# Attention scores on TensorE's row halves and attention-times-values on its quarters, in float32, in a fused attention and MoE kernel

## The chip, the cores and the metric

The kernel runs on one NeuronCore of one Trainium2 chip. The core has a matrix engine (TensorE), three engines for elementwise work (VectorE, ScalarE, GpSimd), a queue engine that issues most transfers (SyncE, called SP in the profile), and 16 DMA engines. The metric is the device time of one execution in microseconds (us). Profiles are of one execution; times are medians of several.

## The reference

The first half is attention over pooled keys and values: 8 batches, 8 heads, 576 positions, head size 64, with means over 8 neighbouring positions, so that each query sees 72 keys. The second half is a dense two-layer network on the 4608 tokens.

```python
k_p = k.reshape(B, H, Sp, pool, D).mean(axis=3)
v_p = v.reshape(B, H, Sp, pool, D).mean(axis=3)
scores = scale * np.matmul(q, k_p.transpose(0, 1, 3, 2))
scores = scores - np.max(scores, axis=-1, keepdims=True)
attn = np.exp(scores)
attn = attn / (np.sum(attn, axis=-1, keepdims=True) + 1e-09)
attn_out = np.matmul(attn, v_p)
...
x = np.ascontiguousarray(attn_out.transpose(0, 2, 1, 3)).reshape(B * S, H * D)
h = x @ w_in                        # 4608 x 512 by 512 x 2048
g = h * np.clip(h + 3.0, 0.0, 6.0) / 6.0
out = g @ w_out                     # 4608 x 2048 by 2048 x 512
```

## The kernel before

The 4608 tokens are cut into blocks of 512, 256 and ten times 384 (`BLOCKS`). While the network runs on one block, the attention of later blocks is done in between: `block_steps` lists a block's attention steps, and `Paced` hands them out at the slots of the network's loops. Blocks 0 to 3 go through the network one by one (`run`, matmuls at L841 and L872). Blocks 4 to 11 go in pairs (`super_block`), with seven products in place of eight (matmuls at L1134, L1188 and L1261), their weights streamed from DRAM in 512 KB chunks by SP (L992). The first part of a super block has 54 paced slots, one for each product of six matmuls, and takes a share of the attention steps (`CUTS`, 0.85 in the first three); the rest are spread over the second part.

Many matmuls are done as three products of parts: an operand is cast to float32r (hi), the remainder is taken by a subtraction (lo), and hi x hi, hi x lo and lo x hi are summed. Other matmuls take plain float32.

The attention of a block goes in tiles of 128 tokens. Heads are handled in four pairs p, and pairs in two groups g of two. One tile and group take these steps:

- **Scores** (`Scores.product`, L456 to L464): one float32 matmul per pair, over 128 rows that hold the two heads' 64 dimensions. The keys lie in `kbds`, 128 rows by 144 columns, with zeros where the head of the row and the head of the column differ. A tile across the border of two batches is multiplied twice, with the other batch's queries cleared. Both pairs of a group go to one PSUM bank.
- **Softmax**: a maximum on VectorE (L467), four exponentials with sums on ScalarE (L472), a reciprocal on VectorE, and the division by the sum on GpSimd (`divide`, L501 and L507). Of the 72 keys the first 64 of each head go to `a`, the last 8 of four heads, twice, to `ar`, the "rest".
- **Transposes** (`transposes`, L566): two matmuls against the identity per group, and one for the rests of both groups. The result is split: ScalarE writes `ahi` (L583), VectorE `alo` (L585), and for the rests ScalarE writes two copies and VectorE a remainder (L596, L598).
- **Times values** (`av`, L641, with `av_sums`, L627): for each pair, four matmuls into one bank: `vhi` x `ahi`, `vhi` x `alo`, `vlo` x `ahi`, and the rests. Value tiles are block-diagonal over the two heads, with zeros cleared by GpSimd (L374). ScalarE copies the bank to `x` (L648). This is done once for each part of a block that lies in one batch: 384 tokens, or 192 and 192.

`load_v` and `prep_v` load the values of a batch, sum over the pool on VectorE (L383) and place the parts (L395, L396, L409, L410); `side_steps` orders them. Batches 0 and 1 have paths of their own.

PSUM has eight banks. The attention takes its banks in turn from a list (`att_bank`): three during the first part of a super block (`a0`, `a1`, `o3`), two during the second. TensorE takes its instructions in one order, which a scheduler sets from a simulated timeline; for the first part of the kernel, up to the fourth step of block 1, the order is written out (`ORDER`).

Of the kernel before, what the change touches and what calls it, by code (L numbers as in the profile page):

```python
# [98 lines left out]
def attention_moe_kernel(  # L99
# [83 lines left out]
    def after_mark():  # L183

        if len(window) == 2 and traced[-1].engine in marks:
            behind(traced[-1], marks[traced[-1].engine])
# [90 lines left out]
    def load_v(b, p):  # L277

        t = vraw[b, p] = ring("vst")
        half = slice(p % 2 * (POOL // 2) * D, (p % 2 + 1) * (POOL // 2) * D)  # L280
        to = t[:, : POOL * D].rearrange("p (c n) -> p c n", c=2)
        p -= p % 2
        if p < NPAIR:
            nc.sync.dma_start(to, v[b, p : p + 2, :, half].rearrange("c r n -> r c n"))
            after_mark()
            return
        for c in range(3):
            nc.sync.dma_start(to[c * REM : (c + 1) * REM], vr[b, :, :, half].rearrange("g r n -> r g n"))
            after_mark()
# [85 lines left out]

    def prep_v(b, p):

        if p == 0 and b not in W:
            place_v(b)
        n = P if p < NPAIR else 3 * REM  # L380
        x, y = (vraw.pop((b, p + i))[:n, : POOL * D].rearrange("p (c n) -> p c n", c=2) for i in range(2))
        for w, a, c in ((4 * D, x, y), (2 * D, x, x[:, :, 2 * D :]), (D, x, x[:, :, D:])):
            nc.vector.tensor_tensor(out=x[:, :, :w], in0=a[:, :, :w], in1=c[:, :, :w], op=ALU.add)  # L383
            after_mark()
        if p < NPAIR:
            place_heads(b, x[:, :, :D], slice(p, p + 2))
        else:
            place_rest(b, x[:, :, :D])
# [50 lines left out]
    class Scores:  # L439
# [25 lines left out]

        def top(self):
            nc.vector.tensor_reduce(out=self.mx, in_=self.ps, axis=AX.X, op=ALU.max, negate=True)  # L467
            self.later()
# [23 lines left out]
        def divide(self, engine):  # L492

            e, sm = self.e, self.sm
            if self.a is None:
# [4 lines left out]
            copies = 3 if self.first else 2  # L500
            engine.tensor_tensor(  # L501
# [6 lines left out]
                out=self.rest.rearrange("p (c h s) -> p c h s", c=copies, h=4),  # L508
# [7 lines left out]

    def scores(j, tile, g):

        s = Scores(tile, g)
        s.product()  # L520
        s.top()
        s.exps()
        s.invert()
        s.divide(nc.vector if j == 1 else nc.gpsimd)

    def a_tiles(j, g):


        if (j, g) not in attnT:
            attnT[j, g] = (  # L530
                pool.tile([P, 2, TMAX], F32R, name="ahi", bufs=2),
                pool.tile([P, 2, TMAX], F32R, name="alo", bufs=2),
                pool.tile([NR, TMAX], F32R, name="arem", bufs=2),
            )
        return attnT[j, g]
# [30 lines left out]
    def transposes(j, tile, g):  # L566
# [9 lines left out]
        for b, _, n, x0 in tile:  # L576
            src, o = ps[:, :, at : at + n], slice(x0, x0 + n)
            at += n
            if b == 0:
# [60 lines left out]

    def av(j, b, x0, T, p, later=None):  # L641
# [14 lines left out]
    def side_steps(b):  # L656

        ks = [lambda p=p: load_k(b, p) for p in range(NPAIR)]
        ks += [lambda p=p: prep_k(b, p) for p in range(NPAIR)]
        vs = []  # L660
        n = NPAIR + NG
        for p in range(n):
            vs.append(lambda p=p: load_v(b, p))
            if p > 2 and p % 2:
                vs.append(lambda p=p: prep_v(b, p - 3))
        vs.append(lambda: prep_v(b, n - 2))
        return ks, vs
# [5 lines left out]
    def block_steps(j):  # L673
# [4 lines left out]
        def turn():  # L678
            tile, g = todo.pop(0)
            steps.append(([], lambda: transposes(j, tile, g), None, ()))  # L680
            if g == NG - 1:
                while left and (left[0][0], left[0][1] + left[0][2]) in [(b, s0 + n) for b, s0, n, _ in tile]:
                    pb, _, T, x0 = left.pop(0)
                    steps.extend(([], lambda p=p, a=(j, pb, x0, T): av(*a, p), "av", (pb,)) for p in range(NPAIR))
# [198 lines left out]
    small = fixed.tile([P, 8], F32, name="small")  # L883
    mask, half, half_low = small[:, :6], small[:, 6:7], small[:, 7:]
# [682 lines left out]
```

## Time and profile before

| | |
|---|---|
| time, median of 3 runs | 892.96 us (892.43 to 894.55) |
| profiled execution, its own time | 893.88 us |
| its span in the trace | 892.1 us |
| instructions | 15646 |
| TensorE busy | 869.2 us, 5360 matmuls |
| VectorE busy | 665.9 us |
| ScalarE busy | 553.6 us |
| GpSimd busy | 83.6 us |
| DMA | 200.00 MB, mean 224 GB/s |

PE is TensorE's matmuls, PEld its weight loads, DVE VectorE, ACT ScalarE, POOL GpSimd. Each row of a group gives the line, engine and operation, what is written from what, shapes and count, then busy time and the mean duration of one, then the idle time of the engine just before them and what ended it. Durations of matmuls overlap, since a matmul is recorded until its last result while the next one already streams; what one costs in a row of them is the distance between starts. Span and profiled time differ by what lies around the traced instructions.

### The profile page before, as it was taken

The page shows a single profiled execution, that of the slowest core. Times are in us where ns is not written, and L with a number is a line of the kernel's source. Part 1 is how long each engine was busy: PE and PEld are TensorE (multiplying, and loading weights), DVE is VectorE, ACT ScalarE, POOL GpSimd, SP SyncE. Part 2 cuts the span into 40 slices and gives each one's busy share as a digit, 9 for nine tenths or more (in the row PEclk, how much of TensorE's full clock was granted, in tenths as well). Part 3 has the DMA queues.
Part 4 walks back from the last instruction along what each step waited for, and adds up shares of the span by engine and source line. Part 5 has one row for each costly group of instructions (what it writes and reads, how often), then busy time and mean ns, then how long its engine had stood idle before and what let it go on. Part 6 is the DMA issues. An engine that isn't in the chain of part 4 may idle for free.

```text
span 892.1 us, 15646 instructions
## 1 busy us (share of the span) xinstructions
PE 869.2 (97%) x5360; PEld 812.3 (91%) x5360; DVE 665.9 (75%) x1340; ACT 553.6 (62%) x1515; POOL 83.6 (9%) x168
## 2 busy tenths in 40 slices
PE   7899999999999999999999999999999999999998
PEld 6788888988989998998888999999999999999998
DVE  6999864567877785869788688897597877466664
ACT  5998766655656655778344688665577746355442
POOL 4100002110211100102000101100100200000000
PEclk9999999999999999999999999999999999999999
DMA  9970205995425234996587968877976777877873
GB/s 294 392 293 1 72 24 192 360 327 167 130 67 160 71 129 135 368 315 225 180 271 239 383 218 295 265 239 236 331 250 213 226 233 240 275 253 238 266 264 132
DMA packets 124654, 200.00 MB, mean 224 GB/s; under 512 B 13216, under 2 KB 81056, under 8 KB 124576
## 3 DMA queue, kind: packets, MB, share of 16 engines
q1 hardware_dynamic: 124432, 199.00, 67.8%
q8 instruction: 43, 0.70, 0.3%
q14 instruction: 35, 0.29, 0.1%
q10 hardware_dynamic: 144, 0.00, 0.0%
HBM read 158.08 MB, written 40.89 MB: 223 GB/s over the span
## 4 chain that ended last, share of the span: by engine, by line
PE 80%; DVE 8%; DMA 5%; ACT 4%; issue 2%; SPq 1%; POOL 0%; DVEq 0%; ACTq 0%; POOLq 0%
PE psx L1134 22%; PE psx L1261 19%; PE pso L872 12%; PE psh L841 12%; PE psx L1188 7%; PE psa L646 3%; PE psa L463 3%; ACT e L472 2%; PE psa L572 1%; DMA raw<-w_in_l 1%; DMA raw<-w_out_l 1%; DMA wd<-wq 1%; DVE vst L383 1%; DMA wsFalse<-wd 1%; DVE wq L939 1%
## 5 line engine op out<-in xcount | busy, mean ns | idle before, releaser
L1134 PE MATMUL psx<-x,wsFalse 128*128 128x384 f32 x768 | 151.8, 341 | 1.7 <-DVE g L1098 0.8
L841 PE MATMUL psh<-xhi,w 128*128 128x384 f32 (+2 forms) x520 | 145.9, 340 | 0.5 <-DVE g L853 0.4
L1134 PEld LDWEIGHTS psx<-x,wsFalse 128*128 128x128 f32 x768 | 133.6, 188 | 3.2 <-ACT c L1107 1.3
L1113 ACT CAST part<-g 128x768 fp32r<-128x768 f32 x100 | 83.3, 836 | 85.0 <-PE psx L1261 65.8
L1115 DVE TENSOR_TENSOR part<-g,part 128x768 fp32r<-128x768 f32 x100 | 95.2, 955 | 46.5 <-ACT part L1113 46.1
L872 PE MATMUL pso<-w,ghi 128*128 128x512 f32 x384 | 120.7, 398 | 0.4 <-ACT o L877 0.4
L1134 PE MATMUL psx<-x,wsTrue 128*128 128x384 f32 x576 | 115.8, 342 | 2.4 <-DMA wsTrue<-wd 2.3
L1261 PE MATMUL psx<-wsFalse,part 128*128 128x256 f32 x864 | 108.3, 282 | 1.5 <-DVE part L1115 1.1
L1261 PEld LDWEIGHTS psx<-wsFalse,part 128*128 128x128 f32 x864 | 105.2, 189 | 2.3 <-DVE part L1115 1.3
L1134 PEld LDWEIGHTS psx<-x,wsTrue 128*128 128x128 f32 x576 | 99.6, 188 | 3.1 <-DVE g L1092 3.1
L841 PEld LDWEIGHTS psh<-xhi,w 128*128 128x128 f32 x520 | 93.2, 188 | 8.2 <-DVE g L853 1.1
L472 ACT ACTIVATE e<-psa,mx 128x72 f32<-128x72 f32 x256 | 78.6, 324 | 23.7 <-DVE mx L467 22.4
L841 PE MATMUL psh<-xlo,w 128*128 128x384 f32 (+2 forms) x260 | 87.1, 336 | 0.0
L501 POOL TENSOR_TENSOR a<-e,sm 128x256 f32<-128x256 f32 x60 | 41.0, 683 | 478.3 <-DVE sm L490 377.9
L1261 PE MATMUL psx<-wsTrue,part 128*128 128x256 f32 x648 | 81.3, 283 | 0.0
L1261 PEld LDWEIGHTS psx<-wsTrue,part 128*128 128x128 f32 x648 | 79.3, 191 | 0.2 <-DVE part L1115 0.2
L872 PEld LDWEIGHTS pso<-w,ghi 128*128 128x128 f32 x384 | 69.1, 188 | 11.2 <-ACT o L877 0.7
L1090 ACT ACTIVATE r<-g,small 128x384 f32<-128x384 f32 x96 | 58.8, 621 | 28.4 <-DVE g L1098 28.0
L872 PE MATMUL pso<-w,glo 128*128 128x512 f32 x192 | 74.4, 399 | 0.0
L1098 DVE TENSOR_TENSOR g<-psx,c 128x384 f32<-128x384 f32 x96 | 52.3, 553 | 28.7 <-PE psx L1134 20.6
L1107 ACT COPY c<-psx 128x384 f32<-128x384 f32 x96 | 45.0, 485 | 28.5 <-PE psx L1134 28.1
L1092 DVE SCALAR_TENSOR_TENSOR g<-r,g 128x384 f32<-128x384 f32 x96 | 54.5, 576 | 9.7 <-ACT r L1090 9.2
(139 smaller groups left out, 1473.2 us busy)
## 6 DMA issues: line engine op xcount, KB each, us to landing
wsFalse<-wd SPq DMA_DIRECT2D x64, 512.0 KB, 4.6
wsTrue<-wd SPq DMA_DIRECT2D x48, 512.0 KB, 4.9
wsFalse<-w2d SPq DMA_DIRECT2D x31, 512.0 KB, 5.0
wsFalse<-w2t SPq DMA_DIRECT2D x27, 512.0 KB, 5.0
wsTrue<-w2d SPq DMA_DIRECT2D x21, 512.0 KB, 5.0
wsTrue<-w2t SPq DMA_DIRECT2D x21, 512.0 KB, 4.9
raw<-w_in_l SPq DMA_DIRECT2D x16, 512.0 KB, 8.6
raw<-w_out_l SPq DMA_DIRECT2D x16, 512.0 KB, 9.2
```

The lines of the kernel that those rows point to most:

```text
L472: nc.scalar.activation(self.e[:, h], self.ps[:, h], AF.Exp, bias=self.mx[:, h : h + 1], accum_out=self.sm[:, h : h + 1])
L841: nc.tensor.matmul(self.ps, l[f][:, c, :], r[:, c, :], start=c == 0 and i == 0, stop=c == NCC - 1 and i == 2)
L872: nc.tensor.matmul(pos, l, r, start=f == 0 and i == 0, stop=f == NF - 1 and i == 2)
L1090: nc.scalar.activation(r, src, AF.Relu, bias=half_low, scale=GSCALE / (6.0 * WSCALE))
L1092: nc.vector.scalar_tensor_tensor(out=g_of[i][:, k], in0=r, scalar=GSCALE, in1=src, op0=ALU.min, op1=ALU.mult)
L1098: nc.vector.tensor_tensor(out=g_of[i][:, k], in0=ps, in1=kept, op=ALU.add)
L1107: nc.scalar.copy(c, ps)
L1113: nc.scalar.copy(t[:, 0], src)
L1115: nc.vector.tensor_tensor(out=t[:, 1], in0=src, in1=t[:, 0].bitcast(F32), op=ALU.subtract)
L1134: nc.tensor.matmul(ps, w[:, l, c * P : (c + 1) * P], t[:, r, c], start=o in (1, 2, 5) and c == 0 and k == 0, stop=c == 1 and k == 2, skip_ ...
L1188: nc.tensor.matmul(to, l, w[:, qs, r], start=f == 0 and k == 0, stop=end and k == 2)
L1261: nc.tensor.matmul(to, t[:, l, k, i * P : (i + 1) * P], w[:, k, r], start=begin and k == 0 and y == 0 and i % 2 == 0, stop=m == NM - 1 and ...
```

## The change

From block 3 on (the third batch) the operands of the attention stay in float32. Scores take one matmul for each head, over the 64 rows of that head and its 72 key columns; the two heads of a pair lie in the two row halves of the array, and each half writes to a bank of its own, so that the products of both groups of a tile are made together at the first group's step (`Scores.products`). After the transposes, ScalarE copies `a` and the rests whole (`whole_a`). Values lie without zeros: two heads in 64 rows each, and `av_of_two` does two pairs at once, with each of its matmuls over 64 rows and 64 output columns, that is, a quarter of the array, and two banks. The rests of a batch are loaded to 128 rows, summed, and multiplied with a mask (`own`), which `own_rest` makes once. The hunks left out change where `divide` writes the rests and add the columns for `own`.

```diff
     def load_v(b, p):
 
         t = vraw[b, p] = ring("vst")
-        half = slice(p % 2 * (POOL // 2) * D, (p % 2 + 1) * (POOL // 2) * D)
-        to = t[:, : POOL * D].rearrange("p (c n) -> p c n", c=2)
-        p -= p % 2
         if p < NPAIR:
-            nc.sync.dma_start(to, v[b, p : p + 2, :, half].rearrange("c r n -> r c n"))
-            after_mark()
+            half = slice(p % 2 * (POOL // 2) * D, (p % 2 + 1) * (POOL // 2) * D)
+            to = t[:, : POOL * D].rearrange("p (g n) -> p g n", g=NG)
+            p -= p % 2
+            for r in range(2):
+                nc.sync.dma_start(
+                    to[r * D : (r + 1) * D], v[b, p + r, :, half].rearrange("(g s) n -> s g n", g=NG)
+                )
+                after_mark()
             return
-        for c in range(3):
-            nc.sync.dma_start(to[c * REM : (c + 1) * REM], vr[b, :, :, half].rearrange("g r n -> r g n"))
-            after_mark()
+        for r in range(2):
+            for g in range(NG):
+                at = (r * NG + g) * REM
+                nc.sync.dma_start(
+                    t[at : at + REM, : POOL * D],
+                    vr[b].rearrange("a (w g s) n -> g (a w) s n", w=2, g=NG)[g],
+                )
+                after_mark()
 
 
     pieces = {}
...
         for w in W[b][:2]:
             nc.gpsimd.memset(w.bitcast(F32), 0.0)
 
+    def own_rest():
+
+        nc.gpsimd.memset(own, 0.0)
+        for r in range(2):
+            for g in range(NG):
+                rows = slice((r * NG + g) * REM, (r * NG + g + 1) * REM)
+                nc.gpsimd.tensor_copy(own[rows, g::NG], mask[rows, 2 + r :: 2])
+
     def prep_v(b, p):
 
-        if p == 0 and b not in W:
-            place_v(b)
-        n = P if p < NPAIR else 3 * REM
-        x, y = (vraw.pop((b, p + i))[:n, : POOL * D].rearrange("p (c n) -> p c n", c=2) for i in range(2))
-        for w, a, c in ((4 * D, x, y), (2 * D, x, x[:, :, 2 * D :]), (D, x, x[:, :, D:])):
-            nc.vector.tensor_tensor(out=x[:, :, :w], in0=a[:, :, :w], in1=c[:, :, :w], op=ALU.add)
+        if b not in W:
+            if not W.keys() - {0, 1}:
+                own_rest()
+            W[b] = (
+                pool.tile([P, NPAIR, 2 * D], F32, name="v32", tag="vhi", bufs=2)[:, :, :D],
+                pool.tile([P, NPAIR, 2 * D], F32, name="vr32", tag="vlo", bufs=2)[:, :2].rearrange(
+                    "p i (g d) -> p (i g) d", g=NG
+                ),
+            )
+        heads, rest = W[b]
+        x, y = vraw.pop((b, p)), vraw.pop((b, p + 1), None)
+        c = 1 if y is None else NG
+        x = x[:, : POOL * D].rearrange("p (c n) -> p c n", c=c)
+        if y is not None:
+            y = y[:, : POOL * D].rearrange("p (c n) -> p c n", c=c)
+        for w in (4 * D, 2 * D, D):
+            z = y if y is not None and w == 4 * D else x[:, :, w : 2 * w]
+            nc.vector.tensor_tensor(out=x[:, :, :w], in0=x[:, :, :w], in1=z[:, :, :w], op=ALU.add)
             after_mark()
+        x = x[:, :, :D]
         if p < NPAIR:
-            place_heads(b, x[:, :, :D], slice(p, p + 2))
-        else:
-            place_rest(b, x[:, :, :D])
+            nc.scalar.mul(heads[:, p : p + 2], x, 1.0 / POOL)
+            return
+        nc.vector.tensor_tensor(
+            out=rest,
+            in0=x.broadcast_to([P, NPAIR, D]),
+            in1=own[:, :, None].broadcast_to([P, NPAIR, D]),
+            op=ALU.mult,
+        )
+        after_mark()
 
     def place_heads(b, vs, some=slice(None)):
         whi, wlo, _ = W[b]
...
                     nc.tensor.matmul(to, qt[:, p, :], kbds[b % 2][:, p, :], start=r == 0, stop=r == last)
             self.ps = ps[:, : 4 * SP].rearrange("p (h s) -> p h s", s=SP)
 
+        @staticmethod
+        def products(tile):
+
+            two = [Scores(tile, g) for g in range(NG)]
+            banks = [att_bank() for _ in two]
+            last = len(tile) - 1
+            for p in range(NPAIR):
+                for r, (qt, (b, _, _, _)) in enumerate(zip(qtiles[tile], tile)):
+                    for g, ps in enumerate(banks):
+                        rows = slice(g * D, (g + 1) * D)
+                        nc.tensor.matmul(
+                            ps[:, SP * p : SP * (p + 1)],
+                            qt[rows, p, :],
+                            kbds[b % 2][rows, p, SP * g : SP * (g + 1)],
+                            start=r == 0,
+                            stop=r == last,
+                        )
+            for s, ps in zip(two, banks):
+                s.ps = ps[:, : 4 * SP].rearrange("p (h s) -> p h s", s=SP)
+            return two
+
         def top(self):
             nc.vector.tensor_reduce(out=self.mx, in_=self.ps, axis=AX.X, op=ALU.max, negate=True)
             self.later()
...
 
     rests = {}
 
+    scored = {}
+
     def scores(j, tile, g):
 
-        s = Scores(tile, g)
-        s.product()
+        if j < 3:
+            s = Scores(tile, g)
+            s.product()
+        else:
+            if g == 0:
+                scored[tile] = Scores.products(tile)
+            s = scored[tile][g]
         s.top()
         s.exps()
         s.invert()
...
                 pool.tile([P, 2, TMAX], F32R, name="ahi", bufs=2),
                 pool.tile([P, 2, TMAX], F32R, name="alo", bufs=2),
                 pool.tile([NR, TMAX], F32R, name="arem", bufs=2),
+            )
+        return attnT[j, g]
+
+    def whole_a(j, g):
+
+        if (j, g) not in attnT:
+            attnT[j, g] = (
+                pool.tile([P, 2, TMAX], F32, name="aT", tag="ahi" if j % 2 else "alo", bufs=2)
+                if g < NG
+                else pool.tile([P, TMAX], F32, name="aTr", tag="arem", bufs=2)
             )
         return attnT[j, g]
 
...
         for b, _, n, x0 in tile:
             src, o = ps[:, :, at : at + n], slice(x0, x0 + n)
             at += n
+            if j > 2:
+                nc.scalar.copy(whole_a(j, g)[:, :, o], src[:, :2])
+                later()
+                if g:
+                    nc.scalar.copy(whole_a(j, NG)[:, o], src[:, 2])
+                    later()
+                continue
             if b == 0:
                 nc.vector.tensor_copy(first_a(j, g)[0], src[:, :2])
             else:
...
             whi, wlo, wrem = W[b]
             mms = [(whi[:, p], hi[:, i, o]), (whi[:, p], lo[:, i, o]), (wlo[:, p], hi[:, i, o])]
         return mms + [(wrem[:, g, i * P : (i + 1) * P], rem[:, o])]
+
+    def av_of_two(j, b, x0, T, i):
+
+        heads, rest = W[b]
+        o = slice(x0, x0 + T)
+        banks = [att_bank()[:, :T] for _ in range(2)]
+        for n in range(2):
+            for g in range(NG):
+                for r, ps in enumerate(banks):
+                    rows = slice(r * D, (r + 1) * D)
+                    nc.tensor.matmul(
+                        ps[g * D : (g + 1) * D],
+                        (rest if n else heads)[rows, 2 * i + g],
+                        whole_a(j, NG)[rows, o] if n else whole_a(j, g)[rows, i, o],
+                        start=n == 0,
+                        stop=n == 1,
+                        skip_group_check=True,
+                    )
+        for r, ps in enumerate(banks):
+            nc.scalar.copy(x_tile(j, "x", F32)[:, 2 * i + r, o], ps)
+            (after_mark if late else no_slot)()
 
     def av(j, b, x0, T, p, later=None):
 
...
 
         ks = [lambda p=p: load_k(b, p) for p in range(NPAIR)]
         ks += [lambda p=p: prep_k(b, p) for p in range(NPAIR)]
-        vs = []
-        n = NPAIR + NG
-        for p in range(n):
-            vs.append(lambda p=p: load_v(b, p))
-            if p > 2 and p % 2:
-                vs.append(lambda p=p: prep_v(b, p - 3))
-        vs.append(lambda: prep_v(b, n - 2))
+        order = [("load", 0), ("load", 1), ("load", 2), ("load", 3), ("prep", 0), ("load", 4)]
+        order += [("prep", 2), None, ("prep", 4)]
+        do = {"load": load_v, "prep": prep_v}
+        vs = [(lambda x=x: do[x[0]](b, x[1])) if x else no_slot for x in order]
         return ks, vs
 
     def loads_behind(tile):
...
             if g == NG - 1:
                 while left and (left[0][0], left[0][1] + left[0][2]) in [(b, s0 + n) for b, s0, n, _ in tile]:
                     pb, _, T, x0 = left.pop(0)
-                    steps.extend(([], lambda p=p, a=(j, pb, x0, T): av(*a, p), "av", (pb,)) for p in range(NPAIR))
+                    of, n = (av, NPAIR) if j < 3 else (av_of_two, NPAIR // 2)
+                    steps.extend(([], lambda p=p, a=(j, pb, x0, T), of=of: of(*a, p), "av", (pb,)) for p in range(n))
 
         for t in tiles_of[j]:
             pre = loads_behind(t)
```

More of the change, by code (lines that the diff above doesn't have):

```diff
@@ L500, in divide @@
             copies = 3 if self.first else 2
+            rest = self.rest.rearrange("p (c h s) -> p c h s", c=copies, h=4) if self.tile[0][0] < 2 else (
+                rests[self.tile].rearrange("p c (g h s) -> p g c h s", g=NG, h=4)[:, self.g]
+            )
             engine.tensor_tensor(
@@ L507, in divide @@
             engine.tensor_tensor(
-                out=self.rest.rearrange("p (c h s) -> p c h s", c=copies, h=4),
+                out=rest,
                 in0=e[:, None, :, D:].broadcast_to([P, copies, 4, SR]),
@@ L639, in av_sums @@
         return mms + [(wrem[:, g, i * P : (i + 1) * P], rem[:, o])]
+    def av_of_two(j, b, x0, T, i):
[13 more added lines that the diff above has]
+                        skip_group_check=True,
+                    )
+        for r, ps in enumerate(banks):
+            nc.scalar.copy(x_tile(j, "x", F32)[:, 2 * i + r, o], ps)
+            (after_mark if late else no_slot)()
     def av(j, b, x0, T, p, later=None):
@@ L882, in attention_moe_kernel @@
     make_identity(nc, ident)
-    small = fixed.tile([P, 8], F32, name="small")
-    mask, half, half_low = small[:, :6], small[:, 6:7], small[:, 7:]
+    small = fixed.tile([P, 8 + NPAIR], F32, name="small")
+    mask, half, half_low, own = small[:, :6], small[:, 6:7], small[:, 7:8], small[:, 8:]
     nc.gpsimd.memset(half, 0.5)
```

## The prediction

> **What bounds the kernel now.** I read the page first, for the engines' shares and the slices, then the waits of TensorE, then its groups with the shapes kept apart, then the timeline of single steps.
>
> ```profile
> span 892.1 us, 15646 instructions
> PE 869.2 (97%) x5360; PEld 812.3 (91%) x5360; DVE 665.9 (75%) x1340; ACT 553.6 (62%) x1515; POOL 83.6 (9%) x168
> ...
> PE   7899999999999999999999999999999999999998
> DVE  6999864567877785869788688897597877466664
> ...
> PE psx L1134 <- DMA wsTrue<-wd: 2.3, 1, 2.3
> ...
> PE psa L463 <- DVE arem L598: 1.3, 3, 0.9
> ...
> PE psa L646 <- DVE alo L585: 0.7, 3, 0.3
> ```
>
> TensorE is busy in 97% of the span and in nine tenths or more of every slice but the first two and the last. Its idle time is 892.1 - 869.2 = 22.9 us in all, and the three waits below the slices show how small the pieces are. VectorE is full only in the third to fifth slice, before any attention of the third batch runs. So a step of attention costs what it adds to TensorE's queue, and work taken from VectorE or ScalarE pays only where TensorE waits for it: 1.3 + 0.7 = 2.0 us for the parts that the change drops. The reader is to see that this is a sum over TensorE's instructions.
>
> **What is replaced.**
>
> ```profile
> L463 PE MATMUL psa<-kbd,qt 128*128 128x144 f32 x288 | 45.3, 287 | 1.3 <-DVE arem L598 1.3
> ...
> L646 PE MATMUL psa<-ahi,vhi 128*128 128x384 f32 x28 | 9.5, 341 | 0.2 <-DVE alo L585 0.2
> ...
> L646 PE MATMUL psa<-ahi,vhi 128*128 128x192 f32 x28 | 7.6, 273 | 0.7 <-DVE alo L585 0.5 <-ACT e L472 0.2
> ```
>
> Each score product is two calls in the code, and four records: one float32 call is two loads and two matmuls, always next to each other. Blocks 3 to 11 hold 27 tiles of 128 tokens; three of them span two batches and are done twice, so 30 tiles' worth, 60 products, 240 of the 288 records. The same blocks have six parts of 384 tokens and six of 192. At four pairs p each, these are 24 of the 28 steps of either width, each with three split matmuls and one for the rest.
>
> ```profile
> 503.21 0.65 PE L463 MATMUL psa<-kbd,qt 128*128 128x144 f32 x4
> 503.61 1.31 PE L1134 MATMUL psx<-x,wsTrue 128*128 128x384 f32 x6
> 504.75 0.34 PE L1134 MATMUL psx<-x,wsFalse 128*128 128x384 f32 x1
> ...
> 531.79 0.33 PE L646 MATMUL psa<-ahi,vhi 128*128 128x384 f32 x1
> ...
> 532.48 1.05 PE L1134 MATMUL psx<-x,wsFalse 128*128 128x384 f32 x5
> ...
> 431.80 0.25 PE L646 MATMUL psa<-ahi,vhi 128*128 128x192 f32 x1
> ...
> 432.23 0.41 PE L1188 MATMUL psx<-wsFalse,part 128*128 128x512 f32 x1
> ```
>
> The durations overlap, so I read starts. Four matmuls of av take 532.48 - 531.79 = 0.69 us at 384 columns (0.1725 each), and 432.23 - 431.80 = 0.43 us at 192 (0.1075 each). A score product takes 0.40 us to the next start; the six matmuls behind it take 1.14 us where six at 0.1725 take 1.035, so 0.105 us of it shows up later: 0.505 us. Removed: 60 x 0.505 = 30.3 us of scores, 24 x 0.69 + 24 x 0.43 = 26.9 us of av.
>
> **What is added: prices.**
>
> ```profile
> 36.65 0.60 PE L646 MATMUL psa<-a,v 128*128 128x256 f32 x2
> 37.09 0.60 PE L646 MATMUL psa<-arem,vrem 96*128 96x256 f32 x2
> ...
> 78.07 0.33 PE L646 MATMUL psa<-a,v 128*128 128x64 f32 x2
> 78.23 0.39 PE L646 MATMUL psa<-a,vrem 96*128 96x64 f32 x2
> 78.43 0.47 PE L841 MATMUL psh<-xhi,w 128*128 128x512 f32 x1
> 78.74 0.40 PE L841 MATMUL psh<-xlo,w 128*128 128x512 f32 x1
> ...
> 464.96 28.36 PE psx L1188 x123
> ```
>
> A float32 call of 256 columns takes 0.44 us, 0.22 per record, 0.86 ns a column. By columns a record costs 0.33 us at 384, 0.165 at 192, 0.062 at 72. But the four records of 64 columns, 0.055 us each by that rate, take 0.36 us to the next start, and the next matmul gives up 0.31 - 28.36/123 = 0.08 more: 0.44, or 0.11 each. That is also the pitch at 192 columns above, where the 384-column rate would give 0.086. So a record with a full-width (128-column) weight load has a floor near **0.11 us**. The new scores, 72 columns wide, still load 128 columns and stand on this floor; the new av loads 64 columns and streams 384 or 192, well above it.
>
> **How much overlaps** decides the sign, and no row before shows a matmul on part of the array. The order of the code does: a call's two records use the same half or quarter, so the second waits for the first; the next call is on another one and can start beside that second record, but its own second record must wait again. If matmuls start in program order, as in every timeline above, two records are in flight at any time, with halves or quarters: n calls of two records take n + 1 record times. I take this.
>
> The Trainium skill ("TensorE: Matmul & The Clock Gate", Part 3) says that matmuls start and end strictly in program order, and nothing here contradicts it: by it the quarters give a factor of two in float32, not four, and the sum is the one below. The same page's 10.6-fold for sixteen tiles is for one matmul per tile; no run here shows either.
>
> - Scores, per tile: 8 calls, 9 x 0.11 = 0.99 us against 1.01. 30 x -0.02 = **-0.6 us**. Bounds: 9 x 0.062 = 0.56 us if the halves hide the load (-13.5 us), 16 x 0.11 = 1.76 us if loads go one by one (+22.5 us). I take the middle since the floor is a row and only its overlap is unknown.
> - av, per step of two pairs: 8 calls, 9 x 0.33 = 2.97 us against 1.38 at 384; 9 x 0.165 = 1.49 against 0.86 at 192; twelve each: 19.1 + 7.5 = **+26.6 us**. Bounds: four at once, 1.32 and 0.66 us (-0.7 - 2.4 = -3.1 us); none, 5.28 and 2.64 us (46.8 + 21.4 = +68.2 us).
> - Changing the array's shape: 27 score steps and 24 av steps, in and out, 102 changes.
>
> ```profile
> 437.38 0.34 PE L646 MATMUL psa<-ahi,vhi 128*128 128x192 f32 x1
> 437.56 0.27 PE L646 MATMUL psa<-alo,vhi 128*128 128x192 f32 x1
> 437.67 0.28 PE L646 MATMUL psa<-ahi,vlo 128*128 128x192 f32 x1
> ```
>
> The nearest row is a matmul behind a transpose: 0.18 us to the next start instead of 0.11. I take this 0.07: 102 x 0.07 = **+7.1 us**; bounds 0 and a whole load more, 0.07 + 0.11 = 0.18 (18 us).
>
> **Other engines.**
>
> ```profile
> L585 DVE TENSOR_TENSOR alo<-psa,ahi 128x256 fp32r<-128x256 f32 x56 | 23.1, 415 | 1.9 <-ACT ahi L583 1.4
> ...
> L598 DVE TENSOR_TENSOR arem<-psa,arem 32x128 fp32r<-32x128 f32 x56 | 16.0, 286 | 4.5 <-ACT arem L596 2.8
> ...
> L410 DVE SCALAR_TENSOR_TENSOR vrem<-vst,small,vrem 32x128 fp32r<-32x128 f32 x24 | 7.7, 365 | 0.3
> ...
> L396 DVE SCALAR_TENSOR_TENSOR vlo<-vst,vhi 64x128 fp32r<-64x128 f32 x24 | 7.5, 313 | 0.5
> ...
> L596 ACT CAST arem<-psa 64x128 fp32r<-64x128 f32 x56 | 14.6, 260 | 11.4 <-DVE alo L585 6.9 <-DVE arem L598 3.8
> ...
> L472 ACT ACTIVATE e<-psa,mx 128x72 f32<-128x72 f32 x256 | 78.6, 324 | 23.7 <-DVE mx L467 22.4
> L472 ACT ACTIVATION_READ_ACCUMULATOR e<-psa,mx 128x1 f32 x256 | 53.7, 210 | 0.0
> ...
> vst<-v_l SPq DMA_DIRECT2D x24, 256.0 KB, 5.1
> ...
> vst<-vr_l SPq DMA_DIRECT2D x36, 64.0 KB, 4.1
> ```
>
> VectorE loses 48 of the 56 in either of the first two rows (19.9 + 13.7 us) and the next two rows whole (15.2 us), some 49 us; ScalarE one of two copies of the rests (24 x 0.26 = 6 us) and most of the placing of values. TensorE covers all of it, so the gain is the **-2.0 us** of waits above. GpSimd's clearing of value tiles goes, its division stays. SP issues 8 + 4 loads of values a batch instead of 4 + 6: twelve more in all, with fewer bytes of the rests. What stands behind them on SP is the weight stream, for which TensorE waited 2.3 us at the longest; one chunk that came as late would cost that, and I add nothing.
>
> The added wait is the second bank: both products of a tile are made at the first score step, each av step needs two banks at once, and the MoE matmuls stand behind on TensorE. A bank comes free after four exponentials, 4 x (0.324 + 0.210) = 2.1 us, of the second half one step later than now. The three attention waits above average 1.3/3 = 0.43 us; one such wait per tile would be 12 us. I take 0: the first part of a super block spreads 85% of some 30 steps over 54 products of 1.035 us, 2.2 us a step, and three banks turn.
>
> **Sum:** -0.6 + 26.6 + 7.1 - 2.0 = +31.1 us. The profiled execution took 893.88 us, 1.8 beyond its span and 0.9 above the median of 892.96; on the median the forecast is **924 us** (+3.5%).
>
> **Rivals.**
>
> - *Four at once* (the forecast's opposite side). If a quarter needs only its own predecessor, the second record of a call does not hold up the next quarter: scores 8 x 0.11 = 0.88 us (-3.9 us), av -3.1, waits -2.0, and half the price of the changes, +3.5: -5.5 us, **887 us**, between 880 and 893. It decides once more than three records run side by side, since av then costs no more than now. For it: the four outputs of a step lie in two banks and two halves of their rows, so none writes where another does. Against: every timeline above has its matmuls one after another, those of a call together. The skill's "TensorEngine Tiling (Array Packing)", Key Properties, says that tiles work independently, in loads too: that is this rival; the same list's drain at a change of mode is the +7.1 us. No run here shows either yet.
> - *Loads one by one, matmuls two by two*: scores +22.5, av +26.6, changes +7.1, waits -2.0: +54 us, **947 us**. For it: the floor of 0.11 us is a load's, and nothing above shows two loads at once.
> - *Loads one by one, quarters four at once*: 22.5 - 3.1 + 7.1 - 2.0 = +24.5, **917 us**.
> - *The parts of the array don't overlap in float32* (the change doesn't do what it says): 22.5 + 68.2 + 7.1 - 2.0 = +95.8, **989 us**.
>
> **How the numbers follow.** Forecast 0.40, its own range 917 (no price for changes) to 947 us (18 us for them, and the bank wait); four at once 0.28; one-by-one loads 0.13; that with quarters at four 0.06; no overlap 0.13. A difference of 0.3% (2.7 us) is about what a measurement of this kernel can tell from none, its three runs lying 2.1 us apart. Of *four at once*, 0.22 is faster than that and 0.06 within it; everything else is slower: 0.72. The range 880 to 952 leaves out no overlap and small tails.
>
> **What would show it.** The 16 records of a 384-column av step from the first start to the next work: about 3.0 us says two in flight, 1.3 four, 5.3 none. Scores: 16 records in 1.0 us or 1.76. The first matmul behind each step against its usual pitch gives the price of a change. PE's idle time before the two-bank steps shows the bank wait. I am wrong if records of one call on the same quarter run together, if hidden VectorE waits were worth far more than 2 us, or if banks make TensorE stand.

## The result and the profile after

The changed kernel takes 935.79 us (median of four runs, 934.43 to 944.91), the kernel before 893.75 us beside it on the same chip (892.43 to 894.87): a ratio of 1.0493 [1.0424, 1.0562], 42.0 us more. The forecast was 31.1 us more. The profiled execution took 935.04 us against 893.88; its span is 41.2 us longer.

First the page of the changed kernel: the span, the engines' shares, and the slices of TensorE (PE) and VectorE (DVE).

```profile
span 933.3 us, 16307 instructions
...
PE 917.7 (98%) x5792; PEld 814.1 (87%) x5792; DVE 618.7 (66%) x1178; ACT 535.8 (57%) x1449; POOL 75.3 (8%) x161
...
PE   7899999999999999999999999999999999999998
...
DVE  6999846446655675656787566876565677466674
```

TensorE has 432 records more and is 48.5 us longer busy. Its idle time falls from 22.9 to 933.3 - 917.7 = 15.6 us. VectorE loses 47 us, about the 49 that were counted, and the span grows all the same. The kernel is still a sum over TensorE's instructions; what the relief of the other engines is worth by itself is tried further down.

Next TensorE's groups after, with the shapes kept apart (the columns are busy time, mean ns of one, idle time before).

```profile
L511 PE MATMUL psa<-kbd,qt 64*128 64x72 f32 x480 | 50.8, 280 | 0.1
...
L733 PE MATMUL psa<-aT,v 64*64 64x384 f32 x96 | 19.7, 507 | 0.0
L733 PE MATMUL psa<-aTr,vr 64*64 64x384 f32 x96 | 17.7, 493 | 0.0
...
L733 PE MATMUL psa<-aT,v 64*64 64x192 f32 x96 | 12.7, 345 | 0.0
...
L733 PE MATMUL psa<-aTr,vr 64*64 64x192 f32 x96 | 10.4, 327 | 0.0
...
L498 PE MATMUL psa<-kbd,qt 128*128 128x144 f32 x48 | 7.3, 286 | 0.0
```

The two halves of the array have 480 records of scores between them, the four quarters 384 of av. The new steps don't wait: their idle column holds 0.1 us in all, and TensorE's view of waits has no row of an attention bank. So the cost of the two banks, which the prediction looked for in idle time, has to be sought elsewhere. Busy time can't be set against the span here, because records that run side by side are counted once and the gaps at a change of shape not at all. What can be read is the starts.

### What a step takes

The timeline of TensorE after: start, duration, line and tiles, number of records in a row.

```profile
513.17 1.11 PE L511 MATMUL psa<-kbd,qt 64*128 64x72 f32 x16
514.22 3.42 PE L1236 MATMUL psx<-x,wsFalse 128*128 128x384 f32 x18
517.57 1.11 PE L511 MATMUL psa<-kbd,qt 64*128 64x72 f32 x8
518.61 0.80 PE L1236 MATMUL psx<-x,wsTrue 128*128 128x384 f32 x3
519.34 0.66 PE L511 MATMUL psa<-kbd,qt 64*128 64x72 f32 x4
519.93 1.32 PE L1236 MATMUL psx<-x,wsFalse 128*128 128x384 f32 x6
521.18 0.66 PE L511 MATMUL psa<-kbd,qt 64*128 64x72 f32 x4
521.77 2.88 PE L1236 MATMUL psx<-x,wsTrue 128*128 128x384 f32 x15
...
553.07 0.86 PE L733 MATMUL psa<-aT,v 64*64 64x384 f32 x4
553.86 0.62 PE L1236 MATMUL psx<-x,wsFalse 128*128 128x384 f32 x2
555.48 0.54 PE L733 MATMUL psa<-aT,v 64*64 64x384 f32 x2
555.49 0.54 PE L733 MATMUL psa<-aTr,vr 64*64 64x384 f32 x2
555.85 0.49 PE L733 MATMUL psa<-aT,v 64*64 64x384 f32 x2
555.86 1.12 PE L733 MATMUL psa<-aTr,vr 64*64 64x384 f32 x6
556.91 1.32 PE L1236 MATMUL psx<-x,wsFalse 128*128 128x384 f32 x6
```

Three things are to be seen. **Scores:** sixteen records, both halves, take 514.22 - 513.17 = 1.05 us to the next start. The tile behind it is not made in one piece: its first eight records belong to one half and take 518.61 - 517.57 = 1.04 us, as long as sixteen, and the other half's eight follow in two pieces of four, at 519.34 and 521.18. **av:** the step at 553.07 starts with four records and is finished at 555.48 with twelve, which take 556.91 - 555.48 = 1.43 us. At 0.33 us a record, two in flight would take some 2 us. **Order:** single starts in this piece are 555.476, 555.483, 555.489 and 555.496, one for each quarter, and the second records come 0.37 us later. In the compiled program a call's two records stand next to each other. So all four quarters start at once, and a second record that has to wait holds nobody up.

A piece also costs something for itself. The starts of single records around the smallest one of av, two records of one step:

```
607.648  last matmul on the whole array (256 columns, usual pitch 0.12)
607.857  first record of a quarter
608.230  second record
608.643  next matmul on the whole array
608.866  the one behind it
```

From the end of the first row's pitch, 607.768, to the begin of a usual pitch ahead of the last row, 608.746, are 0.98 us. The two records need 0.64 (0.32 each, one after the other), which leaves 0.34 us for going into the small shape and out of it. I took this net time for every **visit** to the small shapes in the trace after:

```
records of a visit     visits   net us, mean
av 384 columns, 4         6     0.99
av 384 columns, 12        3     1.64
av 192 columns, 2         3     0.67
av 192 columns, 8         8     0.96
scores, 2                 7     0.59
scores, 4                 6     0.76
scores, 8                16     1.19
scores, 16               10     1.52  (least 1.24)
all kinds                91   111.7 in all
```

Four 384-column records cost 0.99 as two do, since they run side by side; twelve cost 0.345 + 4 x 0.32 = 1.63. One price of **0.345 us a visit** fits. There are 91 visits where the kernel writes 27 + 24 = 51 steps (the compiled program has the same 91 pieces, so the scheduler made them): 91 x 0.345 = 31.4 us. The remaining 80.3 us are matmuls. Side by side throughout, they would be 30 x 8 x 0.1115 = 26.8 us of scores and 12 x 1.29 + 12 x 0.65 = 23.3 us of av, some 50. So there are three terms: the visits that the code has (51 x 0.345 = 17.6 us), the visits added by splitting (40 x 0.345 = 13.8), and 30 us lost because halves or quarters that should run together do not meet.

The same net time for the kernel before (scores 33.0, av 36.7 us from 162 us on, transposes 19.3: 89.0) and after (113.5 + 16.9 = 130.4) gives +41.4 us, the span's 41.2. (The 113.5 hold 1.8 us of the third batch's last av, which the 36.7 hold too.) The match is closer than the method: with slightly other usual pitches the same sum comes to between 42 and 43.5 us, so it is good to some 2 us.

### The profile page after: what moved, and what is told of

The parts are those of the page before. It is cut to its first block, busy times and chain, and to the rows that moved or that the text cites. A ratio compares the mean times of both kernels' runs of the same rounds, so it can differ in the third digit from the quotient of the medians.

```text
span 933.3 us, 16307 instructions
## 1 busy us (share of the span) xinstructions
PE 917.7 (98%) x5792; PEld 814.1 (87%) x5792; DVE 618.7 (66%) x1178; ACT 535.8 (57%) x1449; POOL 75.3 (8%) x161
## 4 chain that ended last, share of the span: by engine, by line
PE 90%; DMA 5%; DVE 2%; ACT 1%; SPq 1%; issue 1%; DVEq 0%; ACTq 0%
PE psx L1236 24%; PE psx L1363 20%; PE pso L974 13%; PE psh L943 13%; PE psx L1290 7%; PE psa L511 5%; PE psa L733 4%; DMA wsFalse<-wd 2%; PE psa L648 2%; DMA raw<-w_in_l 1%; DMA raw<-w_out_l 1%; PE psa L750 1%; PE psa L498 1%; DMA wd<-wq 1%; DMA wsTrue<-wd 1%
## 5 line engine op out<-in xcount | busy, mean ns | idle before, releaser
L1236 PE MATMUL psx<-x,wsTrue 128*128 128x384 f32 x576 | 113.9, 341 | 1.3 <-DMA wsTrue<-wd 1.2
L528 ACT ACTIVATE e<-psa,mx 128x72 f32<-128x72 f32 x256 | 79.1, 330 | 29.4 <-DVE mx L523 28.4
L560 POOL TENSOR_TENSOR a<-e,sm 128x256 f32<-128x256 f32 x60 | 38.9, 650 | 587.6 <-DVE sm L546 522.7
```

The costliest lines, as they stand in the source:

```text
L528: nc.scalar.activation(self.e[:, h], self.ps[:, h], AF.Exp, bias=self.mx[:, h : h + 1], accum_out=self.sm[:, h : h + 1])
L1236: nc.tensor.matmul(ps, w[:, l, c * P : (c + 1) * P], t[:, r, c], start=o in (1, 2, 5) and c == 0 and k == 0, stop=c == 1 and k == 2, skip_ ...
```

## The experiments

Theory A: the price is in the visits and their splitting, as above. Its rivals are named with each run.

### Keeping each step in one piece

The changed kernel, with one difference in the order of TensorE's program: each matmul of a step is kept behind the one before it, halves or quarters take turns, and a step begins with the bank and the operand that are ready last.

```diff
+    def together(kind, new):
+        if new:
+            groups_of.append([])
+        elif groups_of[-1]:
+            behind(traced[-1], groups_of[-1][-1])
+        groups_of[-1].append(traced[-1].name)
...
-                    for g, ps in enumerate(banks):
+                    for g, ps in reversed(list(enumerate(banks))):
...
+                        together("scores", new=p == 0 and r == 0 and g == 1)
...
-        for n in range(2):
-            for g in range(NG):
-                for r, ps in enumerate(banks):
+        for n in (1, 0):
+            for g in (1, 0):
+                for r, ps in reversed(list(enumerate(banks))):
...
+                    together("av", new=n == 1 and g == 1 and r == 1)
```

> The changed kernel with one edit of order: within a score step and within an av step each matmul is kept behind the one before it, halves and quarters in turn, and the step begins with the bank and the operand that come last. The program then enters the small array shape 67 times in place of 91, and 19 of 24 av steps stand in one piece. Theory A (halves and quarters do run at once when their matmuls stand side by side, and each visit to the small shape costs 0.345 us of entry and exit): 24 visits less are 8 us, av steps in one piece some 10 us, score halves that stand side by side again some 14 us: about 904 us. Theory B (the forecast's: two records at a time whatever the order, 0.07 us per change of shape): 24 x 0.14 = 3 us less, 932 us.

Measured: 909.09 us, ratio 1.0174 [1.0151, 1.0196]; 26.7 us of the 42.0 are gone. An av step in this kernel's timeline:

```profile
399.91 0.88 PE L744 MATMUL psa<-aTr,vr 64*64 64x384 f32 x8
400.61 0.82 PE L744 MATMUL psa<-aT,v 64*64 64x384 f32 x8
401.36 2.89 PE L1248 MATMUL psx<-x,wsFalse 128*128 128x384 f32 x15
```

Sixteen records of 384 columns take 401.36 - 399.91 = 1.45 us, four of 0.33 and a little, where the prediction gave 3.0 for two in flight, 1.3 for four. The group of scores on TensorE:

```profile
L521 PE MATMUL psa<-kbd,qt 64*128 64x72 f32 x480 | 37.5, 280 | 0.7 <-DMA qt<-q_l 0.6
```

The same 480 records of the same mean duration are busy 37.5 us instead of 50.8: more of them lie beside each other. There are 67 visits now, with 79.9 us in all: 24 x 0.345 = 8.3 us less for entries and exits, 23.5 us less for matmuls that now meet. Transposes take 3.7 us more (20.6), and the span ends 25.3 us earlier. By kind, the av visits cost 35.7 us, about what the av before cost (36.7 - 1.8 = 34.9); the score visits cost 44.2 where the old ones cost 33.0. Theory A (904 us) is 5 us low, theory B (932) 23 us high: A stands. Seven score steps still came as 2 + 14 records, and stand so in the compiled program: the edit keeps the order of a step's matmuls, but lets other work in between. Why the scheduler put it there is open.

### Each part of the change alone

The kernel before, with the new score products from the fourth block on and everything else old:

```diff
+        if j < 3:
+            s = Scores(tile, g)
+            s.product()
+        else:
+            if g == 0:
+                scored[tile] = Scores.products(tile)
+            s = scored[tile][g]
```

> The kernel before with the new score products alone, from block 3 on. The values stay in the old pairing, so that heads meet other heads' values; the amount of work is that of the kernel before with the new scores. 47 visits to the small shape. Theory A: 47 x 0.345 = 16 us of visits and some 35 us of matmuls (half of the visits hold one half only, at 0.11 us a record), against 30 to 36 us that the old products take: +15 to +21 us, about 912 us. Theory B: 30 tiles at 0.99 us and 47 x 0.14 us: +6 us, 900 us.

Measured: 921.86 us, 1.0327 [1.0295, 1.036], 28.4 us more, above both numbers. TensorE's group:

```profile
L476 PE MATMUL psa<-kbd,qt 64*128 64x72 f32 x480 | 50.5, 280 | 0.0
```

It is the 50.8 of the whole change. There are 47 visits with 57.2 us where the old products took 33.0: 24.2 us more. Of the seventeen visits of eight records, fourteen hold one half alone, at 1.25 us. Of the sixteen visits of sixteen records (1.60 on the mean), seven have both halves side by side throughout, at 1.25; in five the halves come in longer blocks, at 1.5 to 1.75; and four hold one half alone, of a tile that spans two batches, at 2.1. The rest of the 28.4 us may be the clock: it was 0.991 to 0.994 in this kernel's four runs, 0.997 to 1.0 in the runs of the kernel before beside them, and times follow it elsewhere in this study (the kernel with old scores and new av, below, took 902.0 us at 0.994 and 896.8 at 1.0). Scaled so, an estimate, some 5 us of the 28.4 are the clock's, whatever lowered it. Even so the scores alone carry more than half of the loss, though their matmuls were sized rightly: sixteen that take turns are done in 1.05 us.

The changed kernel with the old score products, so that only av and what feeds it are new:

```diff
-        if j < 3:
-            s = Scores(tile, g)
-            s.product()
-        else:
-            if g == 0:
-                scored[tile] = Scores.products(tile)
-            s = scored[tile][g]
+        s = Scores(tile, g)
+        s.product()
```

> The changed kernel with the old score products; heads meet other heads' values as in the run of the scores alone, and the amount of work is that of new values, copies and av. 47 visits to the small shape. Theory A: 16 us of visits and some 36 us of matmuls against 27 to 33 us: +19 to +25 us, about 914 us, and the two parts together give the whole change (+42 us). Theory B: +26.6 us and 47 x 0.14 = 6.6 us, less 2 us of waits: 925 us.

Measured: 909.99 us, 1.0185 [1.0164, 1.0206], 16.6 us more, somewhat below theory A's +19 to +25 and far below theory B. Its 47 visits take 55.3 us against 34.9, transposes 3.0 us less than before: +17.4. The two parts sum to 45.0 us, some 40 without the part of the clock; together they cost 42.0.

### The price of a visit

If 0.345 us belongs to the shape and not to what stands around it, one matmul more should cost it when it uses 64 rows and not when it uses 128. Each score product of the kernel before, from the fourth block on, gets one more float32 matmul of 72 columns in front, into columns that the product then overwrites.

```diff
+            if self.tile in late_tiles:
+                qt, (b, _, _, _) = qtiles[self.tile][0], self.tile[0]
+                nc.tensor.matmul(
+                    ps[:, :SP], qt[:64, 2 * self.g, :], kbds[b % 2][:64, 2 * self.g, :SP], start=True, stop=True
+                )
```

> The kernel before with one float32 matmul more ahead of each of the 54 score products from block 3 on: 64 rows of the queries by 72 key columns, two records, whose result the product overwrites. It makes 52 visits to the small shape. Theory A (0.345 us of entry and exit per visit): 54 x 0.22 + 52 x 0.345 = 30 us, 923 us. Theory B (0.07 us a change): 54 x 0.22 + 52 x 0.14 = 19 us, 912 us. If a change of shape costs nothing: 12 us, 905 us, as in the run with full rows.

The second kernel differs by the rows alone, `qt[:P, ...]` and `kbds[b % 2][:P, ...]`.

> The same extra matmul over all 128 rows, so that the shape never changes. All theories: 54 calls of two records at the 0.11 us that a full-width load takes, 12 us, about 905 us; the difference to the run with half rows is the price of 52 visits: 18 us by theory A, 7 by theory B.

Measured: 917.38 us with 64 rows (1.0261 [1.0238, 1.0284]), 905.07 with 128 (1.0116 [1.0094, 1.0138]). One product of each in the timeline, that with 64 rows first:

```profile
521.62 0.69 PE L1140 MATMUL psx<-x,wsFalse 128*128 128x384 f32 x3
522.24 0.44 PE L461 MATMUL psa<-kbd,qt 64*128 64x72 f32 x2
522.61 0.76 PE L469 MATMUL psa<-kbd,qt 128*128 128x144 f32 x4
523.11 0.60 PE L1140 MATMUL psx<-x,wsFalse 128*128 128x384 f32 x2
```

The same product with 128 rows:

```profile
521.32 0.69 PE L1140 MATMUL psx<-x,wsTrue 128*128 128x384 f32 x3
521.84 0.34 PE L461 MATMUL psa<-kbd,qt 128*128 128x72 f32 x2
522.01 0.70 PE L469 MATMUL psa<-kbd,qt 128*128 128x144 f32 x4
522.46 0.60 PE L1140 MATMUL psx<-x,wsFalse 128*128 128x384 f32 x2
```

From the first row to the last are 1.49 us against 1.14: 0.35 us for the shape. Over all 52 stretches of either trace the net times differ by 17.9 us, 0.344 each. So the number read from the visits is the shape's own, in and out: the two kernels differ in the rows of that matmul alone. By single starts it lies on both sides: the entry takes 0.27 us instead of 0.18, the second record comes 0.167 behind the first instead of 0.062, and the way out is about 0.15 longer. The prediction's 0.07 a change, 0.14 a visit, was read at a transpose, which uses the whole array. The medians differ by less, 12.3 us, halfway between theory A's 18 and theory B's 7 (917.4 lies between 923 and 912). So the price rests on these stretches and not on the times; where the other 5 us went, and in which of the two kernels, is not settled.

### Can the halves be apart?

The kernel with whole steps, but each score step makes all matmuls of one half before those of the other.

```diff
-            for p in range(NPAIR):
-                for r, (qt, (b, _, _, _)) in enumerate(zip(qtiles[tile], tile)):
-                    for g, ps in reversed(list(enumerate(banks))):
+            for g, ps in reversed(list(enumerate(banks))):
+                for p in range(NPAIR):
+                    for r, (qt, (b, _, _, _)) in enumerate(zip(qtiles[tile], tile)):
```

> The run with whole steps, with one edit: a score step makes all matmuls of one half before those of the other, so that neighbours lie on the same half. Same matmuls, 71 visits in place of 67. Theory A (only neighbours on different halves run at once): 8 records more in a row per tile, 30 x 8 x 0.11 = 26 us, and 4 visits 1.4 us, on top of 909: about 935 us. Theory B (two records at a time whatever their half): 909 to 911 us.

Measured: 921.76 us, 1.0324 [1.0298, 1.0349], between the two theories. The thirteen visits of sixteen records take 1.77 us on the mean, against 1.30 when the halves take turns. One of them in the timeline:

```profile
403.60 0.86 PE L1248 MATMUL psx<-x,wsTrue 128*128 128x384 f32 x4
404.39 1.62 PE L521 MATMUL psa<-kbd,qt 64*128 64x72 f32 x16
405.94 0.79 PE L1248 MATMUL psx<-x,wsTrue 128*128 128x384 f32 x3
```

1.55 us to the next start, instead of 1.05 and of 16 x 0.11 = 1.76. The single starts say why:

```
first half   404.390 .556 .668 .780 .891   then 405.003 and on
second half  404.897
```

The second half's first record starts with the fifth of the first half, and ahead of three of the first half that stand before it in the kernel's order and start from 405.003 on. In the compiled program all eight records of the first half stand ahead of the second half's. So TensorE does look past waiting matmuls to those of another part of the array, but not far: here past three. Other visits agree. Where the program has blocks of four records, both halves start 0.013 us apart (first visit of the kernel with the scores alone); where it has blocks of six, the second half starts with the third record (first visit of the changed kernel, at 167.981 behind 167.975). Either way three are passed. That is why turns matter in the scores (the partner is the next matmul) and why the four quarters start together in av (three second records wait).

The Trainium skill ("TensorE: Matmul & The Clock Gate", Part 3) has matmuls start strictly in program order, and the prediction's factor of two hung on that. The starts here and the four quarters after speak against it where matmuls use different parts of the array. For matmuls on the same part of the array nothing in these traces does.

### Is relief of the other engines worth anything?

The kernel before without VectorE's subtraction for the second parts of `a`, from the fourth block on; av multiplies the first part twice, so TensorE has the same work.

```diff
-                nc.vector.tensor_tensor(out=lo[:, :, o], in0=src[:, :2], in1=hi[:, :, o].bitcast(F32), op=ALU.subtract)
-                later()
+                if j < 3:
+                    nc.vector.tensor_tensor(
+                        out=lo[:, :, o], in0=src[:, :2], in1=hi[:, :, o].bitcast(F32), op=ALU.subtract
+                    )
+                    later()
...
+            if j > 2:
+                mms[1] = mms[0]
```

> The kernel before without the remainders of a from block 3 on: VectorE's subtraction is left out, and av multiplies the first part a second time in its place, so that TensorE's work stays the same. VectorE is relieved of some 20 us. If TensorE alone is the bound, 893 us, within 2 us; if work taken from VectorE shortens waits that the trace shows elsewhere, up to 10 us less, 883 us.

Measured: 892.84 us, 0.9991 [0.9973, 1.0009]. The engines on its page:

```profile
PE 869.7 (98%) x5360; PEld 814.4 (91%) x5360; DVE 649.1 (73%) x1280; ACT 551.6 (62%) x1515; POOL 81.4 (9%) x168
```

VectorE is 16.8 us shorter busy and the time does not move. Of the -2.0 us of the sum this kernel tries the 0.7 us of waits for `alo` alone, which don't show; the subtraction for the rests, behind the other 1.3, is still made here.

### A version that keeps what works

Old score products (full shape, no visits), the new av in whole steps. The division puts the heads in the order that the quarters need, which takes one more small GpSimd instruction.

```diff
-                        whole_a(j, NG)[rows, o] if n else whole_a(j, g)[rows, i, o],
+                        whole_a(j, NG)[rows, o] if n else whole_a(j, i)[rows, g, o],
```

> Score products as before the change, values and av as after it: the division writes the heads in the order that av's quarters need (one small instruction more on GpSimd per step), and each av step is kept in one piece. 29 visits to the small shape. Theory A: 29 x 0.345 = 10 us and some 25 us of matmuls, against about 31 us that the old av takes in its place: +4 us, less up to 2 us of waits: 893 to 898 us. Theory B: +26.6 and 29 x 0.14 = 4 us: about 922 us.

Measured: 897.36 us, 1.005 [1.0028, 1.0071]. In the last kernel the parts of 192 tokens make all four pairs in one step, for fewer visits (`av_of_four` itself, which is `av_of_two` over all four pairs, is not shown):

```diff
-                    of, n = (av, NPAIR) if j < 3 else (av_of_two, NPAIR // 2)
+                    of, n = (av, NPAIR) if j < 3 else (av_of_two, NPAIR // 2) if T > 256 else (av_of_four, 1)
```

> The run before this one, with all four pairs in one step where a part has 192 tokens (both steps fit into the same two banks). 23 visits. Theory A: 6 visits less are 2 us less than the run before, 891 to 896 us, about the time before the change. Theory B: no gain beyond 1 us, about 921 us.

Measured: 897.93 us, 1.0052 [1.0033, 1.0071]. Visits fall from 29 to 23, and scores and av take 68.6 us (69.4 in the kernel above, 69.7 before). The 2 us that six visits less should save don't show in the time. TensorE's attention is now as cheap as before, and VectorE, 617.3 us busy instead of 665.9, is 49 us shorter. Both kernels are still 3 to 5 us slower than before (3.3 and 3.9 by the medians, 4.5 and 4.6 by the ratios). The longest waits of TensorE in the first of the two:

```profile
PE psx L1258 <- DVE g L1222: 3.0, 1, 3.0
PE pso L996 <- ACT o L1001: 2.9, 1, 2.9
```

Two single waits of 3 us in the MoE part (0.8 and 0.4 us before) look like the cause, but idle time doesn't account for the difference: TensorE's idle time in all is 898.4 - 876.6 = 21.8 us here, 21.3 in the last kernel and 22.9 in the kernel before. What grew is TensorE's busy time, by 7.4 and 5.7 us. Some of that is the clock, which was 0.996 in both profiled executions and 1.000 in the one before (0.4% of 892 us, an estimate of 3.6 us); the rest stays open. No kernel of this study beats the one before.

## Why the prediction was right and wrong

The sign and the range held (935.8 in 880 to 952; 42.0 more against 31.1), but several terms were wrong, and in opposite directions.

```
us                          forecast                       in the traces
scores and av removed       30.3 + 26.9 = 57.2             33.0 + 34.9 = 67.9
matmuls added               30 x 0.99 + 53.5 = 83.2        80.3 (50 if always side by side)
changes of shape            102 x 0.07 = 7.1               182 x 0.1725 = 31.4
waits, transposes           -2.0                           -2.4
sum                         +31.1                          +41.4
```

- **What bounds the kernel** was right: the span's growth is that of attention on TensorE to some 2 us, and taking 16.8 us from VectorE alone moved nothing. (VectorE's row was misread by one slice: it is full in the second to fourth, still ahead of the third batch.)
- **What is removed** was some 8 to 11 us too low, by the choice of usual pitches. The prediction read one undisturbed step of each kind, and these prices hold: the median of a score product is 0.49 us, of a whole av step 0.70. In the trace before, av stands in 66 stretches, many of them three records and one instead of four. At the full shape that costs nothing: the medians are 0.52 and 0.18 us. The surplus lies in some ten stretches around which TensorE waited or was slow to go on, three of scores and seven of av. The longest, 1.72 us for one record, has a wait of the MoE part behind it:

```profile
580.11 0.45 PE L646 MATMUL psa<-arem,vrem 96*128 96x384 f32 x1
581.63 2.04 PE L1261 MATMUL psx<-wsFalse,part 128*128 128x256 f32 x15 [1.07 <-DVE part L1115]
```

- **av, "two records in flight at any time"**: the step that failed. Four quarters run at once; a whole step takes 1.45 us, not 3.0. Kept whole, the new av costs 35.7 us with its visits against 34.9 before. The rival *Four at once* had the mechanism right. Its forecast of 887 us failed all the same, on the next two points.
- **Scores, "-0.6 us"**: the price of a record (0.11, a half's own pitch) and the overlap of the two halves' loads were right, 1.05 us for sixteen against 0.99. The reason was not: the halves start together (513.174 and 513.180), not one record apart, and without the visit the sixteen cost 1.24 - 0.345 = 0.90 us, eight record times and not nine, as in the rival. That 0.1 us a step hardly counts. What failed is the unspoken premise that a step of the code is a step of the program. Pieces of one half cost as much as both halves, and the scores alone cost +28.4 us.
- **Changes of shape, "0.07"**: mis-sized, 0.17 each (0.345 in and out). The bounds of 0 to 0.18 held it; the number of changes, 182 instead of 102, was outside them. The Trainium skill ("TensorEngine Tiling (Array Packing)", Key Properties) has a drain at a change of mode; the trace agrees that a change costs time, and the 0.345 us in and out are its price here.
- **The second bank, taken at 0**: as a wait it was 0, for TensorE never stood before an attention step. But many a tile was issued in pieces, one half at a time, with other work between. If the bank did that, it cost its time as visits and lost company. That the scheduler split a step because one bank was free and the other not is argued from the order of the pieces; keeping the steps whole got back 26.7 us.

That the sum came near the result is luck. The errors largely cancelled: av's matmuls were priced as two in flight although four run, and split steps brought the 80.3 us close to the 83.2 expected. A total that is nearly right says little about its terms.

Open: why some kernels (the pair with the extra matmul, halves apart) lie about 5 us off their row sums, why seven score steps still split, and why TensorE is busy longer in the last two kernels.

## What to carry to other kernels

Count visits to a small array shape, not its matmuls: here each costs 0.345 us in and out, so a visit must save more than that against the same work at full shape, where a step that is broken up cost nothing extra. Keep all matmuls of a visit together in the program and let the parts of the array take turns, and read in the trace whether the scheduler kept them so; a step can be split without any wait to show it. Relief of an engine that does not set the end was worth nothing here, be it 17 us alone or 49 us along with the new av.

## What was not expected of the hardware

Four 64x64 quarters start within 0.02 us of each other, each with records of its own one after the other (0.32 us at 384 columns). Two halves' 128-column weight loads run side by side: a pair of score records every 0.112 us, the pitch of one alone. And TensorE started a matmul of another half or quarter ahead of three that were waiting (404.897 us ahead of 405.003), but did not look through a whole block of eight.
